# A new issue order on five queues, and a spectrum stored for one load of 64 partitions

## The chip, the cores and the metric

The kernel runs on one core of a Trainium2 chip. The metric is the device time in microseconds (us) of one execution. A core has five engines that work side by side, each through its own instructions in their order: TensorE (PE: weight load, then matmul), VectorE (DVE), ScalarE (ACT), GpSimd (POOL) and SyncE (SP), which here only issues transfers. Transfers (DMAs) are issued by SP, ACT and GpSimd, and carried out by 16 shared DMA engines. An instruction waits at the head of its engine until the semaphores that it names have been raised; what stands behind it waits too.

## The reference

Two heads on separate inputs, concatenated along the last axis to an output of 1 x 2048 x 1280 in bfloat16.

```python
# A: local dilated attention, S = 2048, D = 640, 32 heads of 20, window 8, dilation 2
qkv = (x @ wqkv).reshape(B, S, 3, H, Dh).transpose(2, 0, 3, 1, 4)
idx = pos[:, None] - (jnp.arange(8) * 2)[None, :]          # negative ones are masked
attn = softmax(einsum(q, k[idx]) * Dh ** -0.5)
a = einsum(attn, v[idx]) @ wo
# B: a state-space convolution, L = 2048, D = 640, N = 192
dt = exp(log_dt);  logdA = dt * (A_re + 1j * A_im);  dB = dt * (B_re + 1j * B_im)
K = einsum("dn,dnl,dn->dl", C_re + 1j * C_im, exp(logdA[:, :, None] * l), dB).real
y = irfft2(rfft2(pad(u)) * rfft2(pad(K)))[..., :L] + u * Dskip
```

## The kernel before

The 640 channels of B are worked on in five steps (`NCH = 5`, the last is `LAST = 4`) of 128. Of each step the convolution kernel K is made from tables: magnitudes `R` (exponentials on ACT, L256), sine tables `TA` and `TX` (phases by matmul at L303 and L307, sines on ACT at L311), and products of these on DVE (`PG`, `Q`, `X` at L332, `Y` at L366), which TensorE sums over N (L380, L385) into `Ksb`. Then come a forward transform (`fwd`, L399 to L408), the product with the spectrum of u (L432) and the first half of the inverse transform (`inverse_a`, L445 and L446), whose result `Z`, real and imaginary parts, goes to DRAM: to `Zd` for steps 0 to 3, to `Z4d` for the last. The second half of the inverse (`Inverse`, matmuls `ps_ib`) runs late, between the attention's last matmuls. It reads `Z` back by quarters of the output: a tile of 96 partitions, of which 0 to 31 hold the real part, 32 to 63 the imaginary part and 64 to 95 the term `u * Dskip` (`UDd`).

The attention runs on TensorE and DVE after the tables: projections (`proj_k`, `proj_q`, `proj_v`), logits, softmax, and `av_step` with the sums `ps_o` and the output projection `ps_op` and `ps_x`.

**The start.** `partB_prep` loads the parameters four times, as quarters of 32 partitions. `B_A_re` is split over two queues: quarters 0 and 2 are issued by ACT, 1 and 3 by SP. From it `decays` makes `alpha`: TensorE multiplies each quarter by a diagonal (`DG`, L163 and L166), one PSUM tile for each quarter (`ps_tr_168`, `_173`, `_178`, `_183` in the order of the quarters), and ACT copies them out (L173). `alpha` is the input of all exponentials of step 0 (`exps_chunk`). In the meantime DVE takes the phases from `B_A_im`, splits them in three bfloat16 parts (`hi`, `mid`, `lo`), and SP and GpSimd move these into the tile `LPA` (L194), from which the phase matmuls read. SP also loads `U` (the input u, four transfers of 640 KB in pieces of 320 bytes) and the constants, of which `T2` is the largest with 1 MB.

**What sets the order.** All code is written in one sequence, and at the end `pin` fixes the order of each engine's instructions from the text table `ORDER`: one string for PE, DVE, ACT, SP and GpSimd, each a list of runs `first+count` in hexadecimal over the instructions in the sequence in which they were written. Semaphore waits follow from the tiles that are read and written. In addition the transfers of SP and ACT take eight semaphores in turn, and a transfer is issued only when the one before it on the same semaphore has landed, about eight places ahead in the queue.

Of the kernel before, what the change touches and what calls it, by code (L numbers as in the profile page):

```python
# [13 lines left out]
bf16 = mybir.dt.bfloat16  # L14
f32 = mybir.dt.float32

NCH = 5
LAST = NCH - 1
# [726 lines left out]
class Inverse:  # L745
# [12 lines left out]
    def load(self, qr, c0=0, c1=NCH):  # L758
        nc = self.nc
        pool, tag = ((self.a2, "Z"), (self.att.a1, "prod"), (self.att.ta, "U"), (self.a2, "Z"))[qr]  # L760
        if c0 == 0:
            self.t[qr] = pool.tile([96, 4, NCH, 16, 32], bf16, name="Z", tag=tag)
        t = self.t[qr]
        some = [(nc.gpsimd, t[64:96].rearrange("p g c l n -> p g (c l n)"), self.UDd[:, qr].rearrange("(g p) c n -> p g (c n)", g=4))]
        for ri in range(2):
            rows = t[32 * ri:32 * ri + 32]
            some.append((nc.sync, rows[:, :, 0:LAST].rearrange("p g c l n -> p g (c l n)"), self.Zd[:, ri, qr].rearrange("(p g) c n -> p g (c n)", g=4)))
        for ri in range(2):
            rows = t[32 * ri:32 * ri + 32]
            src = self.Z4d[:, 2048 * ri + 512 * qr:2048 * ri + 512 * qr + 512]  # L770
            some.append((nc.sync, rows[:, :, LAST].rearrange("p g l n -> p g (l n)"), src.rearrange("(p g) n -> p g n", g=4)))
        for queue, dst, src in some[c0:c1]:
            queue.dma_start(out=dst, in_=src)
# [104 lines left out]
def body(tc, ctx, pools, prm, B_u, B_Dskip, Sd, Zd, Z4d, UDd, A_x, A_wqkv, A_wo, out_a, out_b):  # L878
    nc = tc.nc
# [47 lines left out]
    def z_rows(c):  # L927
        return [Z4d[:]] if c == LAST else [Zd[:, i // 2, i % 2 * 2:i % 2 * 2 + 2, c, :] for i in range(4)]
# [126 lines left out]
    a2 = ctx.enter_context(tc.tile_pool(name="a2", bufs=1, side="right", reuse_waits="tile"))  # L1055
# [59 lines left out]
def kernel(  # L1115
# [16 lines left out]
    nc = tc.nc  # L1132
# [45 lines left out]
```

## Time and profile before

| | us |
|---|---|
| median of 3 runs | 390.82 |
| lowest and highest run | 389.01 and 391.63 |
| profiled execution: its own time, which the page gives as the span from the first to the last instruction | 389.9 |
| busy: PE, DVE, ACT, POOL | 338.0, 356.1, 311.8, 49.9 |
| exponentials on ACT (L256), 169 of them | 57.7 |
| `Y` products on DVE (L366), 60 of them | 102.9 |

The profile is one execution. Its views: the page, the busy time of each engine by stretches, the timeline, the groups of transfers, the waits, and the chain of waits, which goes back from the last instruction to what released each step. "Lnnn" is a line of the kernel before; the changed kernel has the same lines up to L756, and a few more or fewer from there. Rows of the order name tiles with a number where names repeat; these numbers are the same in both kernels where the code is.

### The profile page before, as it was taken

Reading aid. Unit: us, or ns where it says so; the run is one execution under the profiler, and the core shown is the slowest. Engines: PE = TensorE matmul, PEld = TensorE weight load, DVE = VectorE, ACT = ScalarE, POOL = GpSimd, SP = SyncE. Lnnn points to the kernel's source line nnn. Section 1 sums busy time; section 2 is a strip of 40 time slices with the busy share of each in tenths; the row PEclk is TensorE's granted clock in tenths of the full one; section 3 lists DMA queues with packets and bytes.
Section 4 is the critical chain, followed back from the end, with each engine's and each line's share of the span. In section 5 each row is a group of like instructions: output and inputs, shape, how many; then the busy total and the mean of one; then the engine's idle time right before and its main releaser. Section 6 shows DMA issues by size and latency. Waiting matters only on the chain.

```text
span 389.9 us, 18862 instructions
## 1 busy us (share of the span) xinstructions
PE 338.0 (87%) x8677; PEld 250.9 (64%) x8677; DVE 356.1 (91%) x353; ACT 311.8 (80%) x524; POOL 49.9 (13%) x102
## 2 busy tenths in 40 slices
PE   1286989788898899988888999999999997789993
PEld 0275878677787778877777576556656775344561
DVE  8989899997999999999999998999988996897971
ACT  3999999799999999999998766455987746576761
POOL 8545001021000000100000100000030100011220
PEclk9998899699999999999999999999999999788998
DMA  6499304035021410151049662110773589399254
GB/s 161 109 192 208 121 13 163 6 103 121 29 84 34 109 32 31 57 131 40 2 118 152 144 133 71 34 30 2 166 248 100 163 192 204 70 254 282 81 141 110
DMA packets 39471, 43.30 MB, mean 111 GB/s; under 512 B 24768, under 2 KB 33952, under 8 KB 38752
## 3 DMA queue, kind: packets, MB, share of 16 engines
q1 hardware_dynamic: 34384, 29.34, 32.4%
q0 software_dynamic: 4112, 12.22, 11.5%
q8 instruction: 68, 1.11, 1.3%
q10 hardware_dynamic: 896, 0.54, 0.5%
q14 instruction: 11, 0.09, 0.1%
HBM read 19.63 MB, written 14.16 MB: 87 GB/s over the span
## 4 chain that ended last, share of the span: by engine, by line
PE 44%; ACT 25%; DVE 18%; issue 6%; DMA 4%; SPq 2%; POOL 0%; ACTq 0%; DVEq 0%; POOLq 0%
ACT R L256 7%; PE ps_k L553 6%; PE ps_q L571 6%; PE ps_v L584 6%; DVE Y L366 5%; ACT A L408 4%; DVE X L332 4%; PE ps_o L697 3%; ACT A L403 3%; PE ps_k L380 3%; PE ps_k L385 3%; PE ps_op L732 3%; PE ps_l L615 2%; PE ps_ia L445 2%; PE ps_f L399 2%
## 5 line engine op out<-in xcount | busy, mean ns | idle before, releaser
L366 DVE TENSOR_TENSOR Y<-PG 128x3072 bf16<-128x3072 bf16 x60 | 102.9, 1750 | 3.0 <-PE ps_k L385 2.8
L256 ACT ACTIVATE R<-LPB 128x192 bf16<-128x192 f32 (+1 forms) x169 | 57.7, 420 | 0.1
L380 PE MATMUL ps_k<-Y,X 128*32 128x64 bf16 x2176 | 46.9, 240 | 7.0 <-issue 2.7
L385 PE MATMUL ps_k<-Y,X 64*32 64x64 bf16 x2176 | 45.5, 234 | 0.7 <-issue 0.6
L380 PEld LDWEIGHTS <-X 128*32 128x32 bf16 x2176 | 34.8, 117 | 15.4 <-issue 6.8
L408 ACT CAST A<-ps_f 128x1024 bf16<-128x1024 f32 x40 | 40.4, 1038 | 3.5 <-PE ps_f L407 3.4
L385 PEld LDWEIGHTS <-X 64*32 64x32 bf16 x2176 | 32.8, 113 | 8.8 <-issue 1.1
L332 DVE TENSOR_TENSOR X<-R,TX 128x1536 bf16<-128x1536 bf16 x40 | 37.3, 950 | 0.3 <-PE ps_k L385 0.3
L311 ACT ACTIVATE TX<-ps_ph 128x768 bf16<-128x768 int16 x40 | 32.2, 838 | 3.7 <-PE ps_ph L307 3.7
L690 DVE TENSOR_TENSOR prod<-v,atp 128x1536 bf16<-128x1536 bf16 (+3 forms) x32 | 31.6, 1022 | 3.7 <-PE ps_o L697 3.7
L303 PE MATMUL ps_ph<-LPB,LPA 128*64 128x256 bf16 x288 | 29.3, 308 | 4.0 <-ACT A L408 1.3
L311 ACT ACTIVATE TA<-ps_ph 128x768 bf16<-128x768 int16 x30 | 24.3, 843 | 1.8 <-PE ps_ph L307 1.7
L407 PE MATMUL ps_f<-A,T 128*128 128x128 bf16 x320 | 22.3, 217 | 3.3 <-ACT A L408 1.3
L604 DVE TENSOR_TENSOR prod<-qT,kT 128x1024 bf16<-128x1024 bf16 (+1 forms) x16 | 22.9, 1486 | 1.2 <-ACT qT L572 0.8
L584 PE MATMUL ps_v<-xT,wv 128*32 128x512 bf16 x400 | 23.2, 379 | 0.0
L553 PE MATMUL ps_k<-xT,wkq 128*128 128x512 bf16 x100 | 23.1, 380 | 0.0
L407 PEld LDWEIGHTS <-T 128*128 128x128 bf16 x320 | 19.1, 96 | 6.1 <-issue 3.3
L571 PE MATMUL ps_q<-xT,wkq 128*128 128x512 bf16 x100 | 22.6, 379 | 0.0
L446 ACT CAST Z<-ps_ia 128x1024 bf16<-128x1024 f32 x20 | 19.6, 1014 | 3.4 <-PE ps_ia L445 2.2
L401 ACT ACTIVATE A<-ps_f,sign 128x1024 bf16<-128x1024 f32 x20 | 21.5, 1149 | 0.2 <-PE ps_f L399 0.2
L332 DVE TENSOR_TENSOR PG<-R,TA 128x768 bf16<-128x768 bf16 (+1 forms) x30 | 19.8, 685 | 1.8 <-ACT TA L311 1.3
L399 PE MATMUL ps_f<-BD,U 128*64 128x128 bf16 x320 | 21.0, 285 | 0.1
(157 smaller groups left out, 696.1 us busy)
## 6 DMA issues: line engine op xcount, KB each, us to landing
P<-A SPq DMA_DIRECT2D x16, 256.0 KB, 3.1
Zdram<-Z SPq DMA_DIRECT2D x16, 256.0 KB, 3.7
Z<-Zdram SPq DMA_DIRECT2D x8, 512.0 KB, 7.0
U<-in_B_u_dram SPq DMA_DIRECT2D x4, 640.0 KB, 9.5
UDdram<-UD POOLq DMA_DIRECT2D x10, 256.0 KB, 2.7
Z<-UDdram POOLq DMA_DIRECT2D x4, 640.0 KB, 6.7
out_dram<-ysb SPq DMA_DIRECT2D x32, 80.0 KB, 3.9
out_dram<-ob POOLq DMA_DIRECT2D x8, 160.0 KB, 3.4
```

What stands on the lines that cost most here:

```text
L256: exp = lambda o, i, m: nc.scalar.activation(out=o, in_=i, func=ACT.Exp, scale=m)
L311: last = nc.scalar.activation(out=dst, in_=words.rearrange("p b (q e f) -> p b q (e f)", e=8, f=4), func=ACT.Sin, scale=PI_LO / 32768.0)
L332: TT = lambda o, a, b, op: V.tensor_tensor(out=o, in0=a, in1=b, op=op)
L366: nc.vector.tensor_tensor(out=Y[:].rearrange("p q (b a) f -> p q b a f", a=8), in0=fa, in1=gb, op=A.mult)
L380: MM(ps[32 * g:32 * g + 32, t], lhsT=X[:, q, x, :, f], rhs=Ys[k][:, q, :, f], start=(t == 0 and n == 0), stop=False, tile_position=(0, 32 ...
L385: MM(ps[32 * g:32 * g + 32, t], lhsT=X[hb, q, x, :, f], rhs=Ys[k][hb, q, :, f], start=False, stop=(n == len(sets) - 1), tile_position=(64 ...
L407: last = MM(ps[:, kk], lhsT=C["T2"][:, 8 * b + kk, :], rhs=A1[:, :, 8 * b + kk, :], start=(kk % 4 == 0), stop=True, skip_group_check=True)
L408: nc.scalar.copy(out=A1[:, :, 8 * b:8 * b + 8, :], in_=ps[:].rearrange("p k (j g) -> p j k g", g=4))
L553: MM(ps[:, i], lhsT=self.wk[:, kt, 128 * ct:128 * ct + 128], rhs=self.x4[:, kt, 2 * i:2 * i + 2, 256 * hf:256 * hf + 256], start=(kt == 0) ...
L571: MM(ps[:, i], lhsT=self.wq[:, kt, 128 * ct:128 * ct + 128], rhs=self.x4[:, kt, 2 * i:2 * i + 2, 256 * hf:256 * hf + 256], start=(kt == 0) ...
L584: MM(ps[32 * sc:32 * sc + 32, i], lhsT=self.wv[:, kt, d + i::DH], rhs=self.xT[:, kt, 512 * sc:512 * sc + 512], start=(kt == 0), stop=(kt = ...
L690: nc.vector.tensor_tensor(out=p2.rearrange("p (d i) -> p d i", i=ni), in0=self.v2[:, 4 * j0:4 * j0 + 4 * nj, off:off + ni], in1=at[:, w, i ...
```

## The change

`Zd` and `Z4d` get the real/imaginary axis in front of the 128 partitions, so that partitions 0 to 63 of a `Z` tile (real part, then imaginary part) are one regular pattern in DRAM. A quarter's load is then three transfers on SP: steps 0 to 3 for two of the four column groups, the other two, and the last step, each over 64 partitions. Before they were four: steps 0 to 3 and the last step, for the real and for the imaginary part, each over 32 partitions. GpSimd's load of `UDd` is cut in two halves of two column groups. The number and the bytes of the stores stay. All five strings of `ORDER` are replaced.

```diff
-    def load(self, qr, c0=0, c1=NCH):
+    def load(self, qr, k0=0, k1=5):
...
-        some = [(nc.gpsimd, t[64:96].rearrange("p g c l n -> p g (c l n)"), self.UDd[:, qr].rearrange("(g p) c n -> p g (c n)", g=4))]
-        for ri in range(2):
-            rows = t[32 * ri:32 * ri + 32]
-            some.append((nc.sync, rows[:, :, 0:LAST].rearrange("p g c l n -> p g (c l n)"), self.Zd[:, ri, qr].rearrange("(p g) c n -> p g (c n)", g=4)))
-        for ri in range(2):
-            rows = t[32 * ri:32 * ri + 32]
-            src = self.Z4d[:, 2048 * ri + 512 * qr:2048 * ri + 512 * qr + 512]
-            some.append((nc.sync, rows[:, :, LAST].rearrange("p g l n -> p g (l n)"), src.rearrange("(p g) n -> p g n", g=4)))
-        for queue, dst, src in some[c0:c1]:
+        ud = self.UDd[:, qr].rearrange("(g p) c n -> p g (c n)", g=4)
+        z = self.Zd[:, :, qr].rearrange("r (p g) c n -> (r p) g (c n)", g=4)
+        z4 = self.Z4d[:, :, 512 * qr:512 * qr + 512].rearrange("r (p g) n -> (r p) g n", g=4)
+        some = [(nc.gpsimd, t[64:96, 0:2].rearrange("p g c l n -> p g (c l n)"), ud[:, 0:2])]
+        some += [(nc.sync, t[0:64, g:g + 2, 0:LAST].rearrange("p g c l n -> p g (c l n)"), z[:, g:g + 2]) for g in (0, 2)]
+        some += [(nc.gpsimd, t[64:96, 2:4].rearrange("p g c l n -> p g (c l n)"), ud[:, 2:4])]
+        some += [(nc.sync, t[0:64, :, LAST].rearrange("p g l n -> p g (l n)"), z4)]
+        for queue, dst, src in some[k0:k1]:
             queue.dma_start(out=dst, in_=src)
...
-    def z_rows(c):
-        return [Z4d[:]] if c == LAST else [Zd[:, i // 2, i % 2 * 2:i % 2 * 2 + 2, c, :] for i in range(4)]
+    def z_rows(c):
+        return [Z4d[:].rearrange("r p n -> p r n")] if c == LAST else [Zd[i // 2, :, i % 2 * 2:i % 2 * 2 + 2, c, :] for i in range(4)]
...
-    LOADS = {(2, 8)[n // NCH] + n % NCH: (2 + n // NCH, n % NCH) for n in range(2 * NCH)}
+    LOADS = {(2, 8)[n // 5] + n % 5: (2 + n // 5, n % 5) for n in range(10)}
...
-    Zd = dpool.tile([128, 2, 4, LAST, 512], bf16, name="Zdram")
-    Z4d = dpool.tile([128, 4096], bf16, name="Z4dram")
+    Zd = dpool.tile([2, 128, 4, LAST, 512], bf16, name="Zdram")
+    Z4d = dpool.tile([2, 128, 2048], bf16, name="Z4dram")
...
-    '2+1 1+1 0+1 3+1 19+1 c+1 7+1 4+1 14+1 6+1 d+1 a+1 9+1 8+1 17+1 1a+1 b+1 e+2 5+1 11+1 10+1 15+1 13+1 12+1 1e+2 18+1 20+1 23+2 1b+2 22+1 21+1 1d+1 16+1 '
+    '0+3 17+1 7+1 5+2 1a+1 8+1 b+1 a+1 14+1 d+1 9+1 c+1 1e+1 19+1 23+1 f+1 16+1 12+2 4+1 e+1 15+1 11+1 24+1 10+1 18+1 1f+1 1b+1 20+1 3+1 1c+2 21+2 25+f '
```

The order at three places, on each engine as it is issued ("x4" is four in a row; a tile's size stands at the end).

SP at the start of the program, before: the two quarters of `B_A_re` among the first transfers.

```order
L123 DMA ldt_105<-in_B_log_dt_dram 32x20 x2
L1140 DMA ident_58<-ident_c 128x128
L132 DMA B_A_re_112<-in_B_A_re_dram 32x5x192
L909 DMA Dn_223<-in_B_Dskip_dram 32x160
L132 DMA B_C_re_138<-in_B_C_re_dram 32x5x192
L140 DMA mix_124<-c_mix 128x288
L132 DMA B_A_re_112<-in_B_A_re_dram 32x5x192
L905 DMA BD_75<-c_BD 128x512
```

The first of them is quarter 1 (partitions 32 to 63), the second quarter 3. After the change the queue begins with `ident`, `ldt`, `Dn`, `mix`, the two tables of `LPB`, `Dn`, and the parameters of B and C, 15 transfers, and goes on, still SP, with these:

```order
L922 DMA U_84<-in_B_u_dram 32x64x160
L917 DMA Dn_223<-in_B_Dskip_dram 32x160
L922 DMA U_84<-in_B_u_dram 32x64x160
L194 DMA LPA_101<-mid_189 32x2x192
L915 DMA T2_76<-c_T2 128x4096
L194 DMA LPA_101<-mid_189 32x2x192
L194 DMA LPA_101<-lo_190 32x2x192
L132 DMA B_A_re_112<-in_B_A_re_dram 32x5x192
L194 DMA LPA_101<-hi_188 32x2x192
L914 DMA EA_77<-c_EA 128x256
L194 DMA LPA_101<-hi_188 32x2x192
L922 DMA U_84<-in_B_u_dram 32x64x160
```

This `B_A_re` is quarter 3. Directly behind these rows, on SP as well, follow:

```order
L194 DMA LPA_101<-lo_190 32x2x192
L917 DMA Dn_223<-in_B_Dskip_dram 32x160
L922 DMA U_84<-in_B_u_dram 32x64x160
L194 DMA LPA_101<-hi_367 32x2x576 x2
L132 DMA B_A_re_112<-in_B_A_re_dram 32x5x192
L194 DMA LPA_101<-mid_368 32x2x576
```

This `B_A_re` is quarter 1. It stood fourth in the queue, and now stands behind all loads of `U` and `T2`.

ACT at the start, before: two transfers, the first table load, the copies of `alpha` (`ps_tr` to `LPB`), and the exponentials `R` of step 0.

```order
L132 DMA B_A_re_112<-in_B_A_re_dram 32x5x192
L141 ACT_TABLE_LOAD
L141 ACTIVATE one_106<-one_106 128x2
L144 ACTIVATE ldt_105<-ldt_105 128x20
L132 DMA B_A_re_112<-in_B_A_re_dram 32x5x192
L173 COPY LPB_102<-ps_tr_168 128x48
L173 COPY LPB_102<-ps_tr_173 128x48
L173 COPY LPB_102<-ps_tr_178 128x48
L173 COPY LPB_102<-ps_tr_183 128x48
L256 ACTIVATE R_231<-LPB_102 128x48x4 x42
L237 CAST cT_167<-ps_tr_433 128x4x48
L256 ACTIVATE R_231<-LPB_102 128x48x4 x3
```

ACT at the same place after the change (`cT` are the coefficients of step 0).

```order
L144 ACT_TABLE_LOAD
L144 ACTIVATE ldt_105<-ldt_105 128x20
L132 DMA B_A_re_112<-in_B_A_re_dram 32x5x192 x2
L173 COPY LPB_102<-ps_tr_173 128x48
L173 COPY LPB_102<-ps_tr_168 128x48
L173 COPY LPB_102<-ps_tr_178 128x48
L173 COPY LPB_102<-ps_tr_183 128x48
L141 ACTIVATE one_106<-one_106 128x2
L256 ACTIVATE R_231<-LPB_102 128x48x4 x17
L237 CAST cT_167<-ps_tr_433 128x4x48
L256 ACTIVATE R_231<-LPB_102 128x48x4 x9
L237 CAST cT_167<-ps_tr_475 128x4x48
```

The copies keep their place ahead of the exponentials; the copies of coefficients stand between the exponentials now. In both kernels TensorE begins with quarter 1, `ps_tr_173`.

TensorE where the second half of the inverse begins, before (`ps_v` is the projection of v, `ps_l` logits, `ps_ib` reads `Z`):

```order
L584 LDWEIGHTS wv_7423
L584 MATMUL ps_v_8995<-xT_6667,wv_7423 32x512
L787 LDWEIGHTS HB_8510
L787 MATMUL ps_ib_9109<-Z_8512,HB_8510 32x480
L787 LDWEIGHTS HB_8510
```

TensorE at the first matmul that reads `Z` after the change:

```order
L615 LDWEIGHTS wv_7423
L615 MATMUL ps_l_8910<-prod_7952,wv_7423 32x256
L786 LDWEIGHTS HB_8510
L786 MATMUL ps_ib_9154<-Z_8512,HB_8510 32x160
L786 LDWEIGHTS HB_8510
```

Before, the first `ps_ib` stands behind the whole of `ps_v_8995` (40 matmuls); now it stands ahead of that block and of the last 24 of the 40 logits `ps_l_8910`.

More of the change, by code (lines that the diff above doesn't have):

```diff
@@ L756, in open_rows @@
         self.ysbs = self.att.a1.tile([128, 4, 8, 160], bf16, name="ysb", tag="qT1")
-    def load(self, qr, c0=0, c1=NCH):
+    def load(self, qr, k0=0, k1=5):
         nc = self.nc
         pool, tag = ((self.a2, "Z"), (self.att.a1, "prod"), (self.att.ta, "U"), (self.a2, "Z"))[qr]
-        if c0 == 0:
+        if k0 == 0:
             self.t[qr] = pool.tile([96, 4, NCH, 16, 32], bf16, name="Z", tag=tag)
         t = self.t[qr]
-        some = [(nc.gpsimd, t[64:96].rearrange("p g c l n -> p g (c l n)"), self.UDd[:, qr].rearrange("(g p) c n -> p g (c n)", g=4))]
-        for ri in range(2):
-            rows = t[32 * ri:32 * ri + 32]
-            some.append((nc.sync, rows[:, :, 0:LAST].rearrange("p g c l n -> p g (c l n)"), self.Zd[:, ri, qr].rearrange("(p g) c n -> p g (c n)", g=4)))
-        for ri in range(2):
-            rows = t[32 * ri:32 * ri + 32]
-            src = self.Z4d[:, 2048 * ri + 512 * qr:2048 * ri + 512 * qr + 512]
-            some.append((nc.sync, rows[:, :, LAST].rearrange("p g l n -> p g (l n)"), src.rearrange("(p g) n -> p g n", g=4)))
-        for queue, dst, src in some[c0:c1]:
+        ud = self.UDd[:, qr].rearrange("(g p) c n -> p g (c n)", g=4)
[6 more added lines that the diff above has]
+        for queue, dst, src in some[k0:k1]:
             queue.dma_start(out=dst, in_=src)
```

115 rows, old and new, of the table ORDER are left out of this document.

## The prediction

> **What bounds the kernel now.** I read the page first, for the span and for who works when.
>
> ```profile
> span 389.9 us, 18862 instructions
> PE 338.0 (87%) x8677; PEld 250.9 (64%) x8677; DVE 356.1 (91%) x353; ACT 311.8 (80%) x524; POOL 49.9 (13%) x102
> PE 44%; ACT 25%; DVE 18%; issue 6%; DMA 4%; SPq 2%; POOL 0%; ACTq 0%; DVEq 0%; POOLq 0%
> ```
>
> No engine is the bound by itself: the chain of waits goes through three of them. So I cut the span into stretches of 20 us and read the busy time of TensorE, VectorE (DVE) and ScalarE (ACT) in each; the columns are the stretch, its length, and the busy time of PE, PEld, DVE, ACT and POOL.
>
> ```profile
> 0.00:20.00 20.00, 4.47 (x54) 3.57 (x56) 18.22 (x51) 13.73 (x53) 14.21 (x29) 1.00 0.56 137
> 100.00:120.00 20.00, 18.85 (x643) 16.36 (x638) 19.59 (x18) 19.98 (x40) 0.72 (x1) 1.00 0.18 56
> 140.00:160.00 20.00, 18.31 (x543) 16.24 (x540) 20.00 (x18) 19.97 (x36) 0.00 (x0) 1.00 0.09 30
> ...
> 260.00:280.00 20.00, 20.00 (x391) 13.66 (x389) 18.62 (x14) 13.21 (x16) 0.13 (x2) 1.00 0.23 56
> 320.00:340.00 20.00, 15.93 (x348) 8.71 (x340) 15.82 (x17) 11.85 (x16) 0.72 (x2) 0.90 0.68 138
> 340.00:360.00 20.00, 18.27 (x407) 9.07 (x391) 17.46 (x18) 13.88 (x26) 2.80 (x5) 0.84 0.99 259
> 360.00:380.00 20.00, 19.89 (x460) 11.66 (x458) 16.52 (x20) 13.33 (x25) 5.16 (x10) 1.00 0.40 116
> ```
>
> In the middle of the convolution (100 to 160 us) ACT and DVE are both full; from there to 320 us TensorE is. A delay that enters before 100 us finds almost nothing to be absorbed in until 320 us. Only the last stage is loose: DVE idles 4.18, 2.54 and 3.48 us there, 10.2 together. So I looked at how the loaded stretch begins, in the timeline of the first 35 us (start, length, engine, line, what, and in brackets the idle time before it).
>
> ```profile
> 4.95 0.10 PEld L163 LDWEIGHTS <-B_A_re 32*128 32x128 bf16 x1 [4.95 <-DMA B_A_re<-in_B_A_re_dram]
> ...
> 7.94 0.20 PE L163 MATMUL ps_tr<-DG,B_A_re 32*128 32x32 bf16 x1 [0.75 <-DMA B_A_re<-in_B_A_re_dram]
> ...
> 8.56 10.73 ACT L256 ACTIVATE R<-LPB 128x192 bf16<-128x192 f32 x42
> ...
> 28.18 0.84 ACT L311 ACTIVATE TA<-ps_ph 128x768 bf16<-128x768 int16 x1
> ...
> 29.12 0.96 DVE L332 TENSOR_TENSOR PG<-R,TA 128x1536 bf16<-128x1536 bf16 x1 [1.16 <-ACT TA L311]
> ```
>
> Read downwards it is one chain. TensorE's first matmuls transpose the four quarters of `B_A_re`; ACT copies them out and starts its exponentials 0.62 us after the last quarter was there (8.56 against 7.94); ACT then works without a gap over 1 us up to the sine table `TA`, and that releases DVE's first table product at 29.12. From there DVE has its main work before it:
>
> ```profile
> 29.12:389.90 360.78, 325.54 (x8506) 240.38 (x8505) 329.97 (x289) 289.79 (x456) 31.16 (x64) 0.96 0.43 108
> ```
>
> **The change part by part. The spectrum loads.** The stores keep their number and bytes. Per quarter of the output SP issues three loads in place of four, and GpSimd two of half the size in place of one.
>
> ```profile
> L773 SPq DMA_DIRECT2D Z<-Zdram x8: 548/592/1261, 308.1 to 353.1; - x8
> L773 POOL DMA_DIRECT2D Z<-UDdram x4: 547/554/560, 308.7 to 349.6; - x4
> ...
> Z<-Zdram SPq DMA_DIRECT2D x4, 512.0 KB, 9.8
> ...
> 321.28 0.38 PE L787 MATMUL ps_ib<-Z,HB 96*32 96x480 bf16 x4
> ```
>
> That is 4 x 0.592 = 2.4 us less issuing on SP and 4 x 0.554 = 2.2 us more on GpSimd, both idle most of the time. The first pair of loads starts at 308.1 and the first matmul that reads `Z` runs at 321.28; with the 9.8 us from issue to landing that this stretch shows, the data is there at about 318.5, so 2.8 us of cover. The new order puts the first of these matmuls ahead of one `ps_v` block (2.33 us for 40 matmuls in this stage), so most of that cover goes. Cost between 0 and 2 us if 64 partitions land no faster, and nothing to gain, as nothing waits for `Z` now. I take 0.
>
> **The start of SP's queue.** This is the term that counts. Two quarters of `B_A_re` are SP's, and before they are its fourth and eighth transfer. Now one is the 23rd and the other, partitions 32 to 63, the 33rd (rows of the order, with repeats counted): behind all four loads of `U`, behind `T2` and behind the pieces of `LPA` that wait for DVE. And TensorE's very first weight load reads exactly those partitions, so that no matmul, hence no copy and no exponential, can start before them. What that costs is read from how SP's queue ran before:
>
> ```profile
> 0.75 0.87 SPq L123 DMA_DIRECT2D ldt<-in_B_log_dt_dram  x2
> ...
> 9.21 1.05 SPq L909 DMA_DIRECT2D Dn<-in_B_Dskip_dram  x2
> ...
> 17.82 2.11 SPq L914 DMA_DIRECT2D U<-in_B_u_dram  x2
> ...
> 24.04 4.97 SPq L914 DMA_DIRECT2D U<-in_B_u_dram  x2
> 29.05 4.48 SPq L194 DMA_DIRECT2D LPA<-hi  x1
> ```
> ```profile
> 29.05 8.30 DMA LPA<-hi
> ```
> ```profile
> U<-in_B_u_dram SPq DMA_DIRECT2D x4, 640.0 KB, 9.5
> T<-c_T SPq DMA_DIRECT2D x1, 1024.0 KB, 5.2
> EA<-c_EA SPq DMA_DIRECT2D x1, 64.0 KB, 2.0
> B_A_re<-in_B_A_re_dram SPq DMA_DIRECT2D x2, 60.0 KB, 2.9
> ```
>
> - First load of `U`: 16 transfers went out between 0.75 and 10.26, 0.59 us each. Now 15 stand ahead of it: 0.75 + 8.9 = 9.7 us.
> - From the first load of `U` to the landing of the transfer queued right behind the fourth took 29.05 + 8.30 - 17.82 = 19.5 us. The same four stand ahead of the late quarter now, and `T2` with them: its 5.2 us less the 2.0 us that the small `EA` took, 3.2 us of data.
> - Landing of the late quarter: 9.7 + 19.5 + 3.2 = 32.4 us.
>
> That sum lets the quarter queue behind the `U` data, as `LPA` visibly did (8.30 us, where an unloaded `B_A_re` takes 2.9). The Trainium skill, page "DMA: Bandwidth & Descriptors", section "Queues, rings and completion order", says that each DMA engine takes descriptors of one issuer in ring order, but that completion is not first in, first out per issuer. By its first half the sum stands, and the 8.30 us agrees; by its second half the quarter could come sooner, which is a rival below.
>
> The bounds come from the row that follows, landing time of `U` (shortest, median, longest).
>
> ```profile
> DMA to landing us min/median/max: 6.0/9.5/13.4
> ```
>
> Early end: two of the `LPA` pieces ahead of the late quarter share a semaphore with `U` and one with `T2`, and are issued only when these have landed. The second `U` is issued at 9.7 + 1.05 + 0.59 = 11.3, lands at 17.3 at the soonest, `T2` 3.2 later at 20.5, five issues of 0.6 bring 23.5, and 2.9 more 26.4 us. Late end: two pairs of `U` at 13.4 each, 9.7 + 26.8 + 2.9 = 39.4 us. I take 32.4.
>
> **ACT up to the first table.** Exponentials start at 32.4 + 0.6 = 33.0, 24.5 us later than 8.56. From there ACT's order up to the same sine table holds 40 exponentials instead of 45 (-5 x 10.73/42 = -1.28), one more sine (+0.81 by the table's own rows below) and one tiny activation (+0.2), the same four copies of coefficients: -0.3.
>
> ```profile
> L311 ACT ACTIVATE TA<-ps_ph x4: 811/822/841, 21.6 to 30.9; 128x768 bf16<-128x768 int16 x4
> ```
>
> So DVE's first product starts 24.2 us later, at 53.3. DVE's work before it does not need `B_A_re` and is done as early as before; it covers nothing, since it was DVE's 26 us of preparation anyway. The gap is new idle time on ACT, TensorE and DVE at once.
>
> **The rest of the order.** Matmuls (8677), ACT table loads (19) and the DVE work are the same in number; what moves is who comes first, in pieces of 8 matmuls instead of 16. From 29.12 on DVE now idles 360.78 - 329.97 = 30.8 us, 5.8 of it behind its last instruction (383.62 + 0.49 to 389.9), so 25.0 us could in principle be won back. The full stretches give next to nothing: the two from 100 and from 140 us have 0.41 and 0.00 us on DVE, 0.02 and 0.03 on ACT. The last stage has 10.2 us; a new order there could return none of it or all, or add as much. I take 4 us back, somewhat under half.
>
> **Sum.** 389.9 + 24.2 - 4.0 = 410.1 us of span. The median of the runs, 390.82, lies 0.9 above the profiled span, so 411 us.
>
> **The rivals.** A measurement of this kernel can tell about 1% from no change, 3.9 us.
>
> *The order swallows the delay (no slower).* Place: DVE's 25.0 us of idle time behind 29.12. If the new order packed all of it, the end would come at 53.3 + 329.97 + 5.8 = 389.1, so about 390; with the early landing too, 384. It decides from 20.3 us won back of the 24.2 (within 1%). For it: the whole order was redone at finer grain. Against: 15 of the 25 us lie in many waits under 4 us per 20 us, with another engine full beside them. Time 386 to 395, chance 0.10.
>
> *The late quarter does not queue.* By the median landing of `U`, the second is there at 11.3 + 9.5 = 20.8, `T2` at 24.0, and five issues on, at 27.0, the quarter is issued; it lands after its own 2.9 us, at 29.9. Time 411 - 2.5 = 408.5. The second half of the page's rule above speaks for it. For: its transfers are small. Against: the 8.30 us of `LPA` in the same place. Chance 0.14.
>
> *SP stalls on issue as well.* SP was held 4.97 and 4.48 us while `U` was in flight. If both stalls fall ahead of the late quarter and `U` takes its longest, landing is at 39.4, and 411 + 7.0 = 418. For: those two rows. Against: the loads of `U` now stand further apart. Chance 0.13.
>
> *The change does not do what it says*, in that the wide load lands no sooner: possible, but then the time moves by the 0 to 2 us above at most. It changes no chance.
>
> **How the numbers follow.** Forecast as summed, 0.63; it is the likeliest, so 411. The range leaves out the rival of the other side and part of the late end: low from the early end of landing (26.4, 6 us less) with 10 us won back in place of 4, 411 - 6 - 6 = 399, taken to 398 for a mixture; high 418. All cases but the first rival are slower by more than 1%; that rival I split 0.07 within 1%, 0.03 faster and none slower, and give 0.01 each to what I did not see. Slower 0.88, same 0.08, faster 0.04.
>
> **What would show it.** In the profile of the changed kernel: TensorE's first weight load on L163 waits for `B_A_re` until about 32 us; ACT's busy time in the first 20 us falls from 13.73 to under 3; the first exponential (L256) near 33; DVE's first product (L332, `PG`) near 53, with an idle time before it of about 25 us put down to ACT `TA`; the chain of waits showing `U` or `T2` on SP near its start; and from 100 to 160 us still full ACT and DVE. It is wrong if the first exponential starts before 14 us, if DVE's busy share behind its first product is over 96%, or if waits for `Z` (L786) are among the longest of TensorE's.

## The result and the profile after

| | us |
|---|---|
| before, median of 4 runs | 390.4 |
| changed, median of 4 runs (483.8 to 488.2) | 485.1 |
| ratio, with its 95% interval | 1.245 [1.240, 1.250] |
| profiled execution of the changed kernel: its time and its span | 485.67 and 483.9 |

The changed kernel is 95 us slower; the forecast was 411 us, with a range of 398 to 418. Times from here on are medians of the undisturbed runs: two each for e3 (456.5 and 461.8, so 459, where expectations written after it say 463, the median of all four) and for e9, three or more for the others.

The page after the change:

```profile
span 483.9 us, 18842 instructions
PE 359.5 (74%) x8677; PEld 259.0 (54%) x8677; DVE 357.9 (74%) x353; ACT 314.6 (65%) x524; POOL 51.1 (11%) x106
PE 35%; DVE 27%; ACT 13%; DMA 12%; issue 8%; SPq 4%; POOL 0%; ACTq 0%; DVEq 0%; POOLq 0%
```

TensorE, DVE and ACT had the same instructions to run, and DVE's and ACT's busy time grew by less than 3 us; the 94 us of longer span are waiting. TensorE alone is busy 21.5 us longer for the same 8677 matmuls, which the last section comes back to. The stretches (length, then PE, PEld, DVE, ACT, POOL, and granted clock, the share of its full clock that TensorE was given) show where the waiting is:

```profile
0.00:20.00 20.00, 0.00 (x0) 0.00 (x0) 17.90 (x47) 1.50 (x2) 11.24 (x27) 1.00 0.99 196
100.00:120.00 20.00, 14.98 (x512) 12.47 (x507) 15.36 (x18) 14.81 (x23) 2.86 (x4) 0.86 0.33 89
140.00:160.00 20.00, 19.19 (x698) 16.01 (x688) 17.45 (x15) 19.14 (x42) 0.72 (x1) 1.00 0.22 70
240.00:260.00 20.00, 10.13 (x230) 8.78 (x229) 15.21 (x14) 13.04 (x24) 0.51 (x2) 0.85 0.01 2
400.00:420.00 20.00, 14.20 (x268) 9.39 (x264) 13.14 (x12) 7.06 (x11) 3.14 (x6) 0.83 0.73 172
55.20:483.90 428.70, 345.26 (x8487) 249.55 (x8483) 331.81 (x289) 293.17 (x460) 27.94 (x55) 0.90 0.34 84
```

The first row is as forecast, the rest is not: from 240 to 260 us no engine is full. Behind its first product DVE is busy 331.81 of 428.70 us, where before it was 329.97 of 360.78.

The start: first the landing, from the chain of waits (start, length), then rows of the timelines of PE, ACT and DVE:

```profile
28.45 5.27 DMA B_A_re<-in_B_A_re_dram
```
```profile
33.77 0.20 PE L163 MATMUL ps_tr<-DG,B_A_re 32*128 32x32 bf16 x2 [33.77 <-DMA B_A_re<-in_B_A_re_dram]
...
35.22 4.41 ACT L256 ACTIVATE R<-LPB 128x192 bf16<-128x192 f32 x17
...
55.20 0.96 DVE L332 TENSOR_TENSOR PG<-R,TA 128x1536 bf16<-128x1536 bf16 x1 [27.04 <-ACT TA L311]
```

DVE's first product comes 26.1 us later than before (55.20 against 29.12). The end comes 94.0 us later (483.9 against 389.9). So 68 us are lost behind the start. These are from the longest waits of the changed kernel (total, how often, longest), and below them stands what before had of the first three:

```profile
PEld L380 <- DVE X L332: 45.5, 12, 7.2
PE ps_k L380 <- DVE X L332: 42.2, 11, 7.0
...
DVE Y L366 <- PE ps_k L385: 34.6, 15, 4.7
...
DVE PG L332 <- ACT TA L311: 31.0, 3, 27.0
...
ACT A L408 <- PE ps_f L407: 22.2, 12, 8.0
...
DVE P L432 <- DMA P<-Sdram: 7.6, 1, 7.6
...
PE ps_ib L786 <- DMA Z<-Z4dram: 5.8, 1, 5.8
```
```profile
DVE Y L366 <- PE ps_k L385: 2.8, 3, 1.3
PEld L380 <- DVE X L332: 2.7, 4, 1.6
...
PE ps_k L380 <- DVE X L332: 1.5, 1, 1.5
```

TensorE's matmuls wait for `X` 11 times, 42.2 us in all, where they waited once, 1.5 us; its weight loads wait 45.5 us in place of 2.7. There are 12 `X` tiles (in the later steps) whose first third is not a product but the sum of the two others, made on DVE by an instruction of its own of 0.95 us, `X<-X` on L332. The first matmuls of a unit read just this third. Two stretches show such a tile (`X_4666` of the order), first of the changed kernel, then of before:

```profile
202.00 0.95 DVE L332 TENSOR_TENSOR X<-X 128x1536 bf16<-128x1536 bf16 x1
...
203.00 0.67 PE L380 MATMUL ps_k<-Y,X 128*32 128x64 bf16 x32 [3.50 <-DVE X L332]
...
208.13 3.43 DVE L366 TENSOR_TENSOR Y<-PG 128x3072 bf16<-128x3072 bf16 x2 [3.52 <-PE ps_k L385]
```
```profile
152.90 0.95 DVE L332 TENSOR_TENSOR X<-X 128x1536 bf16<-128x1536 bf16 x1
...
157.31 0.68 PE L380 MATMUL ps_k<-Y,X 128*32 128x64 bf16 x32 [0.20 <-DVE Y L366]
```

Before, the sum was done 3.5 us ahead of its reader. Now it ends at 202.95 and TensorE starts 0.05 us later, after 3.50 us of waiting; and DVE in turn finds no free `Y` tile and waits 3.52 us for TensorE. Put against the order, 9 of the 12 sums end 0.05 or 0.06 us before the first matmul that reads them (before: 4, by up to 0.12 us). Between the second product of an `X` and its sum DVE's order has 58 other instructions, over all 12, where it had 23; at one place 19, six of them `Y` products of 1.75 us.

### The profile page after: what moved, and what is told of

Same layout as the page of the kernel before. It is cut to its first block, busy times and chain, and to the rows that moved or that the text cites. A ratio compares the mean times of both kernels' runs of the same rounds, so it can differ in the third digit from the quotient of the medians.

```text
span 483.9 us, 18842 instructions
## 1 busy us (share of the span) xinstructions
PE 359.5 (74%) x8677; PEld 259.0 (54%) x8677; DVE 357.9 (74%) x353; ACT 314.6 (65%) x524; POOL 51.1 (11%) x106
## 4 chain that ended last, share of the span: by engine, by line
PE 35%; DVE 27%; ACT 13%; DMA 12%; issue 8%; SPq 4%; POOL 0%; ACTq 0%; DVEq 0%; POOLq 0%
DVE Y L366 8%; DVE X L332 7%; PE ps_k L380 5%; ACT R L256 5%; PE ps_k L385 5%; PE ps_ia L445 3%; DVE PG L332 3%; PE ps_f L399 3%; DMA Zdram<-Z 3%; DMA Z<-Z4dram 3%; PE ps_ph L303 2%; ACT A L408 2%; PE ps_o L697 2%; PE ps_v L584 2%; PE ps_f L407 2%
## 5 line engine op out<-in xcount | busy, mean ns | idle before, releaser
L366 DVE TENSOR_TENSOR Y<-PG 128x3072 bf16<-128x3072 bf16 x60 | 103.9, 1753 | 34.8 <-PE ps_k L385 34.6
L380 PE MATMUL ps_k<-Y,X 128*32 128x64 bf16 x2176 | 46.4, 241 | 43.5 <-DVE X L332 42.2
L380 PEld LDWEIGHTS <-X 128*32 128x32 bf16 x2176 | 33.9, 119 | 51.4 <-DVE X L332 45.5
L256 ACT ACTIVATE R<-LPB 128x192 bf16<-128x192 f32 (+1 forms) x169 | 58.7, 417 | 0.1
L408 ACT CAST A<-ps_f 128x1024 bf16<-128x1024 f32 x40 | 39.9, 1021 | 22.2 <-PE ps_f L407 22.2
L332 DVE TENSOR_TENSOR X<-R,TX 128x1536 bf16<-128x1536 bf16 x40 | 37.0, 951 | 11.9 <-PE ps_k L385 9.9
L332 DVE TENSOR_TENSOR PG<-R,TA 128x768 bf16<-128x768 bf16 (+1 forms) x30 | 20.0, 686 | 31.5 <-ACT TA L311 31.0
L303 PE MATMUL ps_ph<-LPB,LPA 128*64 128x256 bf16 x288 | 31.3, 326 | 2.8 <-ACT TX L311 0.9
L445 PE MATMUL ps_ia<-EA,P 128*128 128x128 bf16 x192 | 23.9, 246 | 6.3 <-DVE P L432 6.1
L163 PE MATMUL ps_tr<-DG,B_A_re 32*128 32x32 bf16 x20 | 1.8, 190 | 35.1 <-DMA B_A_re<-in_B_A_re_dram 33.8
L407 PE MATMUL ps_f<-A,T 128*128 128x128 bf16 x320 | 25.6, 233 | 1.3 <-ACT A L401 1.0
L403 ACT CAST A<-ps_f 128x1024 bf16<-128x1024 f32 x20 | 19.7, 1013 | 8.4 <-PE ps_f L399 8.4
L584 PE MATMUL ps_v<-xT,wv 128*32 128x512 bf16 x400 | 24.3, 397 | 0.0
L407 PEld LDWEIGHTS <-T 128*128 128x128 bf16 x320 | 21.1, 104 | 4.7 <-issue 2.2
L432 DVE TENSOR_TENSOR P<-P,A 128x4096 bf16<-128x4096 bf16 x6 | 13.7, 2290 | 13.3 <-DMA P<-Sdram 7.6
```

The source lines that it names most:

```text
L256: exp = lambda o, i, m: nc.scalar.activation(out=o, in_=i, func=ACT.Exp, scale=m)
L303: MM(o[64 * hh:64 * hh + 64, :, 0:8], lhsT=L[:, 64 * hh:64 * hh + 64], rhs=rhs, start=first, stop=last, skip_group_check=True, tile_positi ...
L332: TT = lambda o, a, b, op: V.tensor_tensor(out=o, in0=a, in1=b, op=op)
L366: nc.vector.tensor_tensor(out=Y[:].rearrange("p q (b a) f -> p q b a f", a=8), in0=fa, in1=gb, op=A.mult)
L380: MM(ps[32 * g:32 * g + 32, t], lhsT=X[:, q, x, :, f], rhs=Ys[k][:, q, :, f], start=(t == 0 and n == 0), stop=False, tile_position=(0, 32 ...
L407: last = MM(ps[:, kk], lhsT=C["T2"][:, 8 * b + kk, :], rhs=A1[:, :, 8 * b + kk, :], start=(kk % 4 == 0), stop=True, skip_group_check=True)
```

## The experiments

Three theories stood at the outset. *The order itself*: the new order of the three compute engines makes waits wherever it starts. *Out of step*: it was packed for an early start, and the late one spoils it. *Transfers*: the late stores and loads on SP and GpSimd lose the time. The edits are given as changes of the five strings of `ORDER` (PE, DVE, ACT, SP, POOL); `_new` is the changed kernel's string, `_old` that of before.

### Start, layout, engines and queues apart

**e1, the two quarters of `B_A_re` first.**

```diff
-'0+3 17+1 7+1 ... 16+1 12+2 4+1 e+1 15+1 11+1 24+1 10+1 18+1 1f+1 1b+1 20+1 3+1 1c+2 ...
+'3+2 0+3 17+1 7+1 ... 16+1 12+2 e+1 15+1 11+1 24+1 10+1 18+1 1f+1 1b+1 20+1 1c+2 ...
```

In SP's string 3 and 4 are quarters 1 and 3.

> Edit: the changed kernel, with only SP's two loads of B_A_re (quarters 1 and 3) put back at the head of SP's queue. The first table product came 26.1 us late in the changed kernel (55.20 against 29.12), and the end 94 us late, so 68 us are lost behind it. Theory 'the order itself': the compute engines' new order loses those 68 us whenever it starts, so only the start comes back: 485.7 - 26 = about 460 (455 to 465). Rival 'out of step': the order was packed for an early start, and the late first table is what makes the engines wait for each other all the way: with the start back, 385 to 400. Rival 'transfers': the late stores and loads on SP and GpSimd lose the 68 us: about 460 as well.

478 us, ratio 1.228 [1.216, 1.239]: 7 us won, not 26. The quarters did land early. But DVE's first product still came at 47.33, as these rows of e1 tell (PE, ACT, DVE):

```profile
29.43 0.29 PE L163 MATMUL ps_tr<-mix,CN 32*128 32x128 bf16 x2 [17.46 <-DVE CN L226]
...
31.64 0.32 ACT L237 CAST cT<-ps_tr 128x192 bf16<-128x192 f32 x1 [14.90 <-PE ps_tr L166]
...
47.33 0.96 DVE L332 TENSOR_TENSOR PG<-R,TA 128x1536 bf16<-128x1536 bf16 x1 [17.48 <-ACT TA L311]
```

Behind the late quarter stood a second wait. In the new order ACT copies the coefficients `cT` between its exponentials, TensorE must first transpose `CN` for that, and DVE makes `CN` last in its preparation. ACT sits behind the copy for 14.90 us with exponentials ready to run.

**e2, new layout and loads, old order.**

```diff
-ORDER = (PE_new, DVE_new, ACT_new, SP_new, POOL_new)
+ORDER = (PE_old, DVE_old, ACT_old, SP_old, POOL_old)   # loads of Z and UDd mapped onto the new ones
```

> Edit: the new layout of the spectrum in DRAM and the new loads, with the issue order of before on all five queues (a quarter's two loads of the imaginary part fall away or become the second column half; the two halves of UDd stand where the whole stood). All theories on the order: as before, 390 (388 to 393; the prediction's first term, 0 to 2 us). Rival 'the loads': if 64-partition loads land late, waits for Z appear and the time is over 395.

390.0 us, ratio 1.000 [0.996, 1.004]. With the order of before, the layout and its loads cost and bring nothing; the 95 us come with the order.

**e3 and e4, engines against queues.**

```diff
-ORDER = (PE_new, DVE_new, ACT_new, SP_new, POOL_new)
+ORDER = (PE_new, DVE_new, ACT_new, SP_old, POOL_old)   # e3
+ORDER = (PE_old, DVE_old, ACT_old, SP_new, POOL_new)   # e4, with e1's edit on SP
```

> Edit: the changed kernel's order on TensorE, VectorE and ScalarE, the order of before on SP and GpSimd (so the early load of B_A_re too). 'The order itself': 460 (455 to 465), since the loss sits in the three engines. 'Out of step': 385 to 400. 'Transfers': 385 to 405, as the queues of before are back.

> Edit: the reverse of the run above: the order of before on TensorE, VectorE and ScalarE, the changed kernel's on SP and GpSimd, so that quarter 1 of B_A_re is late. 'The order itself': the start only, 390 + 26 = about 416 (410 to 422). 'Out of step', if it holds for any order that was packed for an early start: over 440. 'Transfers': over 450.

e3: 459 us. 'Transfers' falls as the main cause: with the old queues the new engine order still loses 69 us. 'Out of step' is not decided yet: the quarters are early, but DVE's first product still comes at 45.21, 15.7 us later than in e2 (29.54), since the wait for `CN` is there as in e1. It is decided in e10 and e18.

e4: 416.5 us, ratio 1.066 [1.057, 1.075]. This is the number that 'the order itself' named, but it does not confirm it: the text says that quarter 1 is late, while the kernel that ran had both quarters first. Its 26 us are those of the rest of the two queues. A part is the start, in another way, as the timeline of PE in e4 shows:

```profile
28.94 1.06 PE L303 MATMUL ps_ph<-LPB,LPA 128*64 128x256 bf16 x8 [9.16 <-DMA LPA<-lo]
```

Here the pieces of `LPA` come late, and DVE's first product with them, 12.2 us later than in e2 (41.78 against 29.54). What the late quarters cost was left for e18.

### The late sums

**e5, e9: the sums moved up.** One of the 12 places:

```diff
 L332 X_4666<-R_3230,TX_4017
+L332 X_4666<-X_4666,X_4666
 L366 Y_4853<-PG_4658,PG_4658
 L332 X_4670<-R_3230,TX_4017
 L332 X_4670<-R_3230,TX_4017
 L366 Y_4855<-PG_4658,PG_4658
-L332 X_4666<-X_4666,X_4666
 L366 Y_4857<-PG_4658,PG_4658
```

> Edit: the kernel of e3_new_engines_old_queues (463.0 us), with VectorE's 12 sums that make the first third of an X tile (X<-X,X on L332, 0.95 us each) put directly behind the second of the two products they add; nothing else moves. In e3 TensorE's first ps_k block of a unit waits for this sum 12 times, 42.1 us in all, and 9 of the 12 sums end 0.1 us before that block starts. Theory 'late sums': these 42 us go, 463 - 42 = about 421 (415 to 435). Rival 'split blocks' (TensorE's ps_k blocks of 64 cut in halves with other work between): 455 to 465. Rival 'the waits move on': another wait takes their place, 445 to 460.

435.0 us, ratio 1.118 [1.111, 1.126]: 24 us less than e3. So the sums do bind: 28 of the 42 us of waiting for `X` went, and 24 us of time with them. The waits of e5:

```profile
DVE Y L366 <- PE ps_k L385: 18.3, 9, 4.6
...
PE ps_k L380 <- DVE X L332: 14.4, 6, 4.2
```

DVE's wait for a free `Y` fell with it, from 34.8 us in e3: about half of it was an echo of TensorE's. The 14.4 us left on `X` are taken up in e14.

> Edit: the changed kernel as it is, with only the 12 sums of X on VectorE put directly behind their second product. In e5 the same edit took 463.0 to 435.0. 'Late sums' as a cause of its own: 485 - 28 = 457 (452 to 463) here too, start and queues unchanged. If the late start covers it: 470 or more.

e9, the same edit on the changed kernel itself: 460 us, ratio 1.183 [1.174, 1.193], 25 us less. The late start does not cover it.

**e6, TensorE's blocks joined.** The rival: `ps_k` blocks of 64 matmuls are cut in halves, with other work between.

```diff
 L380 ps_k_4064<-Y_4058,X_3849 x32
+L385 ps_k_4064<-Y_4058,X_3849 x32
 L399 ps_f1_3876<-BD_75,Ksb_2166 x16
 L303 ps_ph_3971<-LPB_102,LPA_101 x8
-L385 ps_k_4064<-Y_4058,X_3849 x32
```

> Edit: the kernel of e3 with TensorE's ps_k blocks joined: the second 32 matmuls (L385) of each of 68 blocks moved up directly behind the first 32 (L380); in e3, 38 of the 68 have other matmuls between, 830 in all. From the first matmul of a block to its last it takes 151 us summed over the blocks in e3, 91 us with the old order. Theory 'late sums': no effect, 455 to 465. Rival 'split blocks': the 60 us of difference are the loss, 405 to 420.

460.6 us, ratio 1.178 [1.168, 1.189]: no effect. The finer grain costs nothing here. In e3's trace the other matmuls between the halves take 59 us: the 60 us by which the blocks take longer are work that has to be done anyway, not time lost by cutting.

**e7 and e8, VectorE's order alone.**

```diff
-ORDER = (PE_old, DVE_old, ACT_old, SP_old, POOL_old)
+ORDER = (PE_old, DVE_new, ACT_old, SP_old, POOL_old)   # e7; e8: and the 12 sums moved up
```

> Edit: the kernel of e2_new_rows_old_order (390.0 us) with VectorE's order of the changed kernel, all other engines and queues in the order of before. Theory 'late sums': most of the loss appears, 415 to 435, with TensorE waiting for X. Rival 'split blocks' (TensorE's order): 390 to 400.

> Edit: the kernel of e7 with the 12 sums put directly behind their second product. Theory 'late sums': back to 390 to 397. If e7 loses by something else in VectorE's order: within 5 us of e7.

e7: 438.3 us, ratio 1.126 [1.118, 1.135], somewhat over the 415 to 435 that were expected. DVE's order alone, on kernels that are otherwise as before, costs 48 us. e8: 412.6 us, ratio 1.060 [1.054, 1.066]. The sums are 26 of the 48; 'back to 390' was too much. Part of the rest is the start, in the rows of PE in e2 and, below, in e8:

```profile
16.61 0.42 PE L163 MATMUL ps_tr<-mix,CN 32*128 32x128 bf16 x4 [7.92 <-DVE CN L226]
```
```profile
27.33 0.28 PE L163 MATMUL ps_tr<-mix,CN 32*128 32x128 bf16 x1 [18.77 <-DVE CN L226]
```

With DVE's new order `CN` reaches TensorE 10.7 us later, and DVE's own first product came at 39.21 for it, 9.7 us later than in e2.

### The start, the queues and what was left

**e10, the start of before.**

```diff
+first = 180 PE, 65 DVE, 74 ACT, 29 SP, 34 POOL   # started by 31 us in the trace of before
-ORDER = order of e5
+ORDER = order of before up to first, then e5's order of the rest
```

> Edit: the kernel of e5 (435.0 us), with the first 31 us of work in the order of before on every engine (what before's trace had started by then), and the changed order for the rest. In e5 the first Q product of VectorE comes 15.7 us later than with the old order (46.2 against 30.5). 'The start slides through': 435 - 16 = 419 (415 to 424). Rival 'the start is absorbed': over 430. Rival 'out of step': under 405.

422.5 us, ratio 1.088 [1.082, 1.094]. DVE's first `Q` product is back to 31.0 us (e2 30.5, e5 46.2), 15.2 us earlier, and the end 12.5 us earlier: it slides through, nearly in full. 'Out of step' (under 405) falls here: with the start of before the rest of the order still loses 32 us, and that with the sums already moved.

**e11, e12 and e16, the queues.**

```diff
 SP, where the last stage begins (e12 against e11):
 L415 Zdram_63<-Z_7901
+L415 P2_8355<-Sdram_62
+L1023 P1_7945<-Sdram_62
+L415 P2_8355<-Sdram_62
 L415 Zdram_63<-Z_7901 x2 ...
-(the same three, one ahead of the four stores, one between, one behind)
```

> Edit: the kernel of e5 with SP's queue in the order of the changed kernel (quarters of B_A_re first), GpSimd in the old one. In the changed kernel SP's three loads of P from the stored spectrum of u stand among the stores of Z, which held SP for 11.94 us; with the changed queues VectorE's last two P products came 13 us later against those before them (69.4 to 82.4 late), with the old ones 5 us (67.4 to 72.7). 'Loads behind stores': 435 + 8 = 443 (440 to 448). Rival 'GpSimd's queue' makes all the difference of the queues: 433 to 438.

> Edit: the kernel of e11 with SP's three loads of P put behind the first of the four stores of Z of step 3, where they stood before; the rest of SP's queue as changed. 'Loads behind stores': back to 433 to 438. If another part of SP's queue costs: as e11.

> Edit: the kernel of e5 (435.0 us) with GpSimd's queue in the order of the changed kernel, SP's in the old one. GpSimd's load of HB stands there behind two loads of UDd, and TensorE waited 6.1 us for HB in the changed kernel. If GpSimd's queue makes the rest of the queues' 17 us: 435 + 9 = 444 (440 to 448). If not: 433 to 438.

e11: 442.5 us, ratio 1.138 [1.133, 1.143], 7.4 us for SP's queue. e16: 435.0, ratio 1.116 [1.109, 1.122]: nothing for GpSimd's. The place that was suspected in SP's queue, in the timeline of SP and DVE in the changed kernel:

```profile
357.09 11.94 SPq L415 DMA_DIRECT2D Zdram<-Z  x3
369.07 0.47 SPq L1023 DMA_DIRECT2D P<-Sdram  x1
...
371.26 0.79 SPq L415 DMA_DIRECT2D P<-Sdram  x1
...
379.19 4.49 DVE L432 TENSOR_TENSOR P<-P,A 128x4096 bf16<-128x4096 bf16 x2 [7.63 <-DMA P<-Sdram]
```

SP stands at the stores of `Z` for 11.94 us, the loads of `P` behind them come late, DVE waits 7.63 us. But e12, which puts them ahead again, took 441.2 us, ratio 1.134 [1.130, 1.138]. DVE's two `P` products began 4.4 us earlier than in e11 (330.74 and 335.18), and the end came 1.3 us earlier, which the intervals don't tell from none: the gain was lost again behind them, so a wait that is seen is not yet time. Of the 7 us, 2.2 are there at the start already (DVE's first product at 47.40 in e11, 45.22 in e5); what else in SP's queue makes them was not found. Nor do the queues add up: 19 us between e1 and e3, 7 + 0 here with the sums out of the way, 26 in e4.

**e13 and e14, cut blocks again, and the products of `X`.** Both on e10; e14 moves 20 instructions of DVE, for instance:

```diff
 L332 X_3853<-R_3230,TX_3265
...
+L332 X_3853<-R_3230,TX_3265
+L332 X_3853<-X_3853,X_3853
 L366 Y_4281<-PG_3841,PG_3841
 L366 Y_4283<-PG_3841,PG_3841
-L332 X_3853<-R_3230,TX_3265
-L332 X_3853<-X_3853,X_3853
 L366 Y_4279<-PG_3841,PG_3841
```

> Edit: the kernel of e10 (423 us) with TensorE's ps_k blocks joined as in e6. If the late sums hid the cost of the cut blocks in e6: 400 to 412. If the cut costs nothing: 420 to 425.

> Edit: the kernel of e10 with 20 of VectorE's instructions that make X moved ahead of the first Y that TensorE reads together with that X; nothing else moves. TensorE still waits for X 6 times in e10, 10.6 us in all. If these waits bind: 423 - 10 = 413 (408 to 417). If other waits take their place: 420 to 428.

e13: 422.2 us, no effect, so the late sums had hidden nothing in e6. e14: 411.3 us, ratio 1.058 [1.052, 1.064], 11 us less; TensorE's wait for `X` is gone from its list. What is left there:

```profile
DVE Y L366 <- PE ps_k L385: 11.6, 5, 4.5
...
PE ps_k L380 <- DVE Y L366: 8.7, 4, 5.1
```

**e17, the rest split.** e14's order on DVE, with PE and ACT in the order of before.

```diff
-ORDER = (PE of e14, DVE of e14, ACT of e14, SP_old, POOL_old)
+ORDER = (PE_old,    DVE of e14, ACT_old,    SP_old, POOL_old)
```

> Edit: the kernel of e14 (412 us) with TensorE and ScalarE in the order of before; VectorE keeps e14's order (start of before, changed order behind it, sums and products of X first). If X and the start are all that VectorE's order costs: 388 to 394, and the 22 us of e14 belong to TensorE's and ScalarE's order. If something else in VectorE's order costs: 400 or more.

400.8 us, ratio 1.028 [1.022, 1.034]. Half of the 21 us belongs to TensorE's and ScalarE's order, half to something else in DVE's; neither was traced further.

**e15, the sums first in the order of before.** e5's edit on e2.

```diff
 ORDER = (PE_old, DVE_old, ACT_old, SP_old, POOL_old)
+DVE: each of the 12 X<-X directly behind its second product
```

> Edit: the kernel of e2 (390.0 us, the order of before) with the 12 sums of X directly behind their second product. TensorE waits for X 2.7 us in all with the order of before, so at most that is to be had: 387 to 390. If a sum put early delays a Y that is waited for: 390 to 393.

392.1 us, ratio 1.008 [1.005, 1.012]: no gain, rather a loss. That the sums of before stood late enough not to hold up a `Y` and early enough for TensorE would fit it; it was not traced. No version was found that beats before.

**e18, the late quarters alone.** What e4 was meant to show, on e2.

```diff
 SP: U_84 x2, Dn, LPA, U_84,
+    B_A_re_112 (quarter 3)
 SP: U_84
+    B_A_re_112 (quarter 1)
-    both among the first eight transfers
```

> Edit: the kernel of e2 (390.0 us, the order of before on all engines and queues), with SP's two quarters of B_A_re moved behind the third and the fourth load of U; nothing else moves. In before's trace the transfer queued right behind the fourth load of U was issued at 29.05 and took 8.30 us, an unloaded quarter 2.9: landing at 32 to 37. 'The start slides through' (the prediction's second and third term): first exponentials at 33 to 38, VectorE's first product 24 to 29 us late, and 390 + 24 to 29 = 414 to 419 at the end. Rival 'absorbed': under 400. Rival 'out of step' (an order packed for an early start loses more than the delay): over 430.

418.8 us, ratio 1.073 [1.065, 1.080], 28.7 us for two transfers of 60 KB that were moved. From the chain of waits and DVE's timeline in e18:

```profile
28.33 8.81 DMA B_A_re<-in_B_A_re_dram
```
```profile
59.55 0.96 DVE L332 TENSOR_TENSOR PG<-R,TA 128x1536 bf16<-128x1536 bf16 x1 [31.58 <-ACT TA L311]
```

The first product is 30.0 us later than in e2 (29.54), the end 28.7 us. The start is 1 us later than was expected of it (24 to 29). Nearly all of the delay comes through, and no more than the delay: 'out of step' (over 430) falls for the order of before too.

### The account

One way from the changed kernel back to before, each step a run:

| step | us | gain |
|---|---|---|
| changed | 485.1 | |
| quarters of `B_A_re` first (e1) | 478 | 7 |
| both queues as before (e3) | 459 | 19 |
| 12 sums first (e5) | 435.0 | 24 |
| first 31 us as before (e10) | 422.5 | 12.5 |
| products of `X` first (e14) | 411.3 | 11 |
| PE and ACT as before (e17) | 400.8 | 10.5 |
| rest of DVE as before (e2) | 390.0 | 11 |

The 19 and the 24 rest on e3, whose two runs lie 5 us apart. Steps taken in another sequence have other sizes: the quarters are worth 7 us here and 28.7 by themselves, since here `CN` and `cT` wait behind them.

## Why the prediction was right or wrong

**Right in direction: slower.** The chance of slower was 0.88; but only 26 of the 94 us lie at the start, where the forecast had its whole loss.

**Right with the order of before, unproven with the new one: the spectrum loads.** The term was 0, with bounds 0 to 2: e2 gives 390.0, none. But the cover of 2.8 us did go, as the prediction said it might, and more: in the changed kernel TensorE waits 5.8 us for the last step's part of `Z`. With the engines' new order that wait is there with SP's new queue (5.7 in e1) and not with the old one (e3). What it costs by itself was not measured.

**Right: the start of SP's queue.** Landing forecast at 32.4, bounds 26.4 to 39.4; it landed at 33.7. By parts it is less exact: `U` began at 9.31 where 9.7 was summed, `T2` took 7.00 us and not 5.2, the quarter was issued at 28.45 and landed in 5.27 us, between the unloaded 2.9 and the 8.30 of `LPA`. The rule of the Trainium skill, page "DMA: Bandwidth & Descriptors", section "Queues, rings and completion order", that completion is not first in, first out per issuer, did not come to bear: the last load of `U` was issued at 24.50 and took 6.7 to 7.6 us, so it was there before the quarter. The rival 'late quarter does not queue' (29.9) and 'SP stalls as well' (39.4) are both off; what held SP there was 3.27 us at two pieces of `LPA`.

**Right by number, incomplete by cause: ACT up to the first table.** Exponentials at 35.22 (forecast 33.0), first product 26.1 us late (forecast 24.2). But the sentence that DVE's work before it "is done as early as before" was wrong in what counts: the work as a whole ends at 28.2 us in place of 28.0, but its first `CN` begins at 26.41 in place of 15.51 and reaches TensorE 10.7 us later (e8), and the "same four copies of coefficients" on ACT now stand between the exponentials. Both hid behind the quarter, so the sum came out right by luck, and undoing the quarter won 7 us.

**Right: it slides through.** The full stretches gave nothing back: e18 loses 28.7 of 30.0 us, e10 wins 12.5 of 15.2.

**Wrong: the rest of the order, and with it the time.** The term was -4 us, with "none of it or all, or add as much" as its bounds, 10.2 us. It was +68. The failing step is that the price of a new order was taken from the idle time of the old trace. That time bounds what an order can win; it bounds nothing of what it can lose. The stretches that were full because each producer ran ahead of its reader were taken as a property of the work ("almost nothing to be absorbed in"), and are one of the order. The material for a bound was there: the order lists the 12 sums behind 58 instructions in place of 23, and the rows of before have 0.95 and 1.75 us for what passes them. Nothing but the start of the order was read so. In place of the 4 us won, the account above has 24 us for the late sums, 11 for late products of `X`, 19 for the queues beside the quarters, and 21 in the order of the engines whose cause stays open.

One reading of the rows of before was off as well, without weight in the sum: TensorE is not full "from there to 320 us". From 160 to 220 us it is busy 17.58 to 18.11 us of each 20, and DVE 19.81 to 20.00.

**Wrong: the signs to look for.** ACT's 1.50 us in the first 20, the exponentials, DVE's 27.04 us of idle time and `T2` in the chain came as written. ACT and DVE full from 100 to 160 us did not (14.81 and 15.36 of 20). Of the signs that would speak against the forecast (busy share over 96%, here 331.81 of 428.70 or 77%; waits for `Z`, 5.8 us where `X` has 42.2) none covered a worse order. The rival 'the order swallows the delay' had the sign of the term wrong, and no rival had a loss in the middle.

## What to carry to other kernels

When an order written out by hand changes, go through each engine's list for the last small producer in front of each large reader, and count what now stands between it and its inputs: 12 instructions of 0.95 us, pushed behind larger products, cost 24 to 26 us in three different settings. Idle time in the old profile bounds the gain of a new order, never its loss. A wait at the start may hide a second one: undo it alone before it gets the whole bill.

## What the runs showed of the hardware

TensorE was busy 359.5 us in the changed kernel and 338.0 before, for the same matmuls. Its granted clock fell from a mean of 0.966 to 0.907, and to 0.85 from 240 to 260 us. A few rows of the changed kernel, by 2 us, show how:

```profile
200.00:202.00 2.00, 0.00 (x0) 0.00 (x0) 2.00 (x3) 2.00 (x5) 0.26 (x1) 1.00 0.39 131
202.00:204.00 2.00, 1.00 (x60) 0.90 (x64) 2.00 (x3) 0.12 (x1) 0.00 (x0) 0.74 0.00 0
204.00:206.00 2.00, 2.00 (x38) 1.90 (x27) 0.61 (x1) 0.00 (x0) 0.00 (x0) 0.50 0.03 8
206.00:208.00 2.00, 2.00 (x74) 1.62 (x72) 0.00 (x0) 1.55 (x3) 0.00 (x0) 0.91 0.01 4
```

TensorE stands still for the 3.50 us of waiting shown above, and just behind it the clock is at half, while it works without a pause. The Trainium skill, page "TensorE: Matmul & The Clock Gate", section "Part 1: The HAM clock gate", says that the clock is halved after an idle window of about 3.4 us and released after as long a stretch of work. The rows agree: the wait was 3.50 us, and the clock is back to 0.91 in the stretch from 206 us on, which begins 3 us after the work did. So this wait was paid twice on TensorE; how many others were long enough for it was not counted. With the sums first TensorE was busy 351.8 us (e5) in place of 356.2 (e3), at a mean clock of 0.957 in place of 0.916. An estimate from the two means of the clock, 338.0 x 0.966 / 0.907 = 360 us, is about the 359.5 that were measured, so the clock can account for all of the longer busy time. How many of the 95 us it makes was not measured by itself.
